# First token tile loaded in two column halves by two queues, and a variance subtraction moved from VectorE to GpSimd, in a fused layer-norm, attention and MLP kernel

## The chip, the cores and the metric

One core of a Trainium2 chip. The time is the device time of one execution in microseconds (us), as the median of several runs. A profile is one execution taken by the hardware profiler; its span is about 1.25 us shorter than that execution's time. All times below that come with no unit are microseconds, and times inside a profile count from the start of its span.

In the lines of profiles, PE is TensorE, PEld its weight loads, DVE VectorE, ACT ScalarE, POOL GpSimd and SPq SyncE's queue. Of the names, `x_tok` holds the token tiles, `bst`, `mv` and `rstd` their statistics, `xnT` the transposed tiles, `WVK` the value weights and `w_s` the MLP weights.

## The reference

```python
def reference(A_x, A_wqkv, A_w_phi, A_wo, B_x, B_w1, B_w3, B_w2):
    x = A_x                                   # [1, 2048, 640], bf16
    xn = _layernorm(x, axis=-1)               # (x - mean) / sqrt(var + 1e-5)
    # _A_ref: qkv projection, 32 heads of 20, a learned feature map with two
    #         softmaxes, linear attention, output projection       ... cut ...
    # _B_ref: (silu(xn w1) * (xn w3)) w2, inner width 1536         ... cut ...
    return x + _A_ref(xn, A_wqkv, A_w_phi, A_wo) + _B_ref(xn, B_w1, B_w3, B_w2)
```

Only the layer norm of the first four token tiles (128 tokens x 640 columns each, 160 KB) and the loads of the first 10 us matter here.

## The kernel before

The kernel is a generator: streams of small steps are emitted in an order chosen from modelled times, and each engine then plays its own list in order, waiting on semaphores. An instruction that waits holds up all that stand behind it on its engine.

The first loads. "SP" is SyncE's queue, "ACT" is ScalarE's. The load of tile 1 reads, in name only, a small zeroed tile, so it waits until VectorE has zeroed it.

```python
    def first_loads():
        load_x(0, 1)                                             # tile 0, SyncE
        o = P.dma("ACT", x_tok[:, 1:2, :], x_t[:, 1:2, :])       # tile 1, ScalarE
        o.reads = P.regions(zero[:])
        P.op("ACT", "activation", [warm[:]], [warm[:]], (warm[:], warm[:], ACT.Exp), cost=1.5)
        load_wv(0, 2)        # value weights, chunks 0 and 1, 320 KB
        load_x(2, 3)         # tile 2
        load_wv(2, 4)        # chunks 2 and 3
        load_wv(4, DC)       # chunk 4, 160 KB
        load_x(3, 4)         # tile 3
        w13(0, 512)          # two loads of 640 KB
        # ... cut ...
```

The statistics of tiles 0, 2 and 3 come from VectorE, those of tile 1 from two ScalarE sums with a mean (`act_mean`) and a subtraction on VectorE. The power for 1/sqrt is GpSimd's.

```python
    def act_rstd(t):
        v, r = mv[:, t, 1:2], rstd[:, t, 0:1]
        small(v, sums[:, 0:1], sums[:, 8:9], ALU.subtract)       # VectorE
        P.op("POOL", "tensor_tensor", [r], [v, mhalf[:, 0:1]], (r, v, mhalf[:, 0:1], ALU.pow), cost=0.6)
```

The order of the first normalisations is also VectorE's order.

```python
        yield lambda: act_sums(1)            # ScalarE
        yield lambda: ln_stats(0, 1)
        yield lambda: act_mean(1)            # VectorE, needs ScalarE's first sum of tile 1
        yield lambda: ln_apply(0, 0, 256)    # tile 0, then its first transposes
        yield lambda: act_rstd(1)
        yield lambda: ln_apply(0, 256, D)
        # ... cut ...
        yield lambda: ln_sums(2, 0)
        yield lambda: ln_apply(1)
        yield lambda: (ln_sums(2, 1), ln_rstd(2, 1))
        yield lambda: ln_sums(3, 0)          # needs tile 3
        yield lambda: ln_apply(2)            # stands behind it
```

The softmax here doesn't subtract the row's maximum and nothing guards it: scores larger than these inputs give would overflow.

## Time and profile before

| | value | where from |
|---|---|---|
| time | 266.33 (266.24 to 266.5) | median of 3 runs |
| span of the profile | 265.1 | page |
| TensorE busy | 260.4, 98% | page |
| first long stretch of TensorE begins | 7.12 | chain of waits |
| first weight load of the MLP (`PS<-xnT,w_s`) | 11.63 | timeline |

The page's first part gives the busy time of each engine; the chain of waits is followed back from the last instruction, so each of its pieces was on the path that set the end. In a timeline line, the brackets at the end give the idle time ahead of an instruction and what ended it; no brackets mean that the engine went straight on. The lines themselves are in the prediction.

### The profile page before, as it was taken

The page shows a single profiled execution, that of the slowest core. Times are in us where ns is not written, and L with a number is a line of the kernel's source. Part 1 is how long each engine was busy: PE and PEld are TensorE (multiplying, and loading weights), DVE is VectorE, ACT ScalarE, POOL GpSimd, SP SyncE. Part 2 cuts the span into 40 slices and gives each one's busy share as a digit, 9 for nine tenths or more (in the row PEclk, how much of TensorE's full clock was granted, in tenths as well). Part 3 has the DMA queues.
Part 4 walks back from the last instruction along what each step waited for, and adds up shares of the span by engine and source line. Part 5 has one row for each costly group of instructions (what it writes and reads, how often), then busy time and mean ns, then how long its engine had stood idle before and what let it go on. Part 6 is the DMA issues. An engine that isn't in the chain of part 4 may idle for free.

```text
span 265.1 us, 4353 instructions
## 1 busy us (share of the span) xinstructions
PE 260.4 (98%) x1716; PEld 141.0 (53%) x1744; DVE 183.0 (69%) x319; ACT 106.9 (40%) x228; POOL 94.4 (36%) x107
## 2 busy tenths in 40 slices
PE   8999999999999999999999999999999999999997
PEld 4655545565558555555545455555544444444773
DVE  4668999999796679989995979897986103221112
ACT  5656988799870445355225245445220000000000
POOL 4311587989995033333330704333420000000000
DMA  7996068923302890445614174366292362461431
GB/s 221 289 315 170 4 157 236 179 52 53 120 2 56 256 213 11 88 73 99 113 27 80 37 123 80 72 123 121 52 110 49 78 149 74 99 198 22 104 124 52
DMA packets 76757, 29.68 MB, mean 112 GB/s; under 512 B 65472, under 2 KB 76736, under 8 KB 76736
## 3 DMA queue, kind: packets, MB, share of 16 engines
q1 hardware_dynamic: 76592, 29.23, 49.3%
q8 instruction: 14, 0.23, 0.4%
q10 hardware_dynamic: 144, 0.16, 0.2%
q14 instruction: 7, 0.06, 0.1%
HBM read 10.84 MB, written 2.62 MB: 51 GB/s over the span
## 4 chain that ended last, share of the span: by engine, by line
PE 95%; DVE 2%; DMA 1%; issue 1%; POOL 0%
PE PS L104 95%; DMA x_tok<-in_A_x_dram 1%; DVE t L104 1%; DVE hT L104 0%; DVE bst L104 0%; POOL rstd L104 0%; DVE mv L104 0%; DVE x_tok L104 0%; DVE xres L104 0%
## 5 line engine op out<-in xcount | busy, mean ns | idle before, releaser
L104 PE MATMUL PS<-xnT,w_s 128*128 128x512 bf16 x464 | 105.5, 379 | 0.9 <-issue 0.2
L104 PEld LDWEIGHTS PS<-xnT,w_s 128*128 128x128 bf16 x480 | 46.2, 98 | 51.4 <-DVE xnT L104 0.3
L104 POOL TENSOR_TENSOR eqt<-eqt,rS 128x600 bf16<-128x600 bf16 (+1 forms) x32 | 41.1, 1305 | 72.4 <-DVE rS L104 72.4
L104 ACT ACTIVATE th<-PS 128x512 f32<-128x512 f32 x48 | 28.6, 596 | 50.7 <-PE PS L104 50.6
L104 PE MATMUL PS<-WVK,xnT 128*128 128x512 bf16 (+4 forms) x255 | 45.1, 329 | 0.3
L104 POOL TENSOR_TENSOR ekt<-ekt,rS 128x640 bf16<-128x640 bf16 x32 | 39.8, 1275 | 4.9 <-DVE rS L104 4.9
L104 DVE SCALAR_TENSOR_TENSOR t<-th,PS 128x512 bf16<-128x512 f32 x48 | 32.0, 668 | 13.7 <-ACT th L104 13.5
L104 PE MATMUL PS<-hT,w_s 128*128 128x512 bf16 x179 | 41.1, 379 | 0.0
L104 ACT ACTIVATE eqt<-PS 128x240 bf16<-128x240 f32 (+1 forms) x96 | 27.2, 348 | 27.7 <-PE PS L104 25.9
L104 PEld LDWEIGHTS PS<-WVK,xnT 128*128 128x128 bf16 x260 | 24.2, 98 | 19.3 <-ACT WVK L104 0.4
L104 DVE SCALAR_TENSOR_TENSOR hT<-t,PS 128x512 bf16<-128x512 bf16 x48 | 33.0, 687 | 1.6
L104 DVE TENSOR_TENSOR xT<-PS,xT 128x512 bf16<-128x512 f32 x15 | 10.1, 685 | 34.7 <-PE PS L104 31.6
L104 PEld LDWEIGHTS PS<-hT,w_s 128*128 128x128 bf16 x180 | 17.6, 98 | 21.3
L104 DVE TENSOR_REDUCE S<-eqt 128x66 f32<-128x1320 bf16 x16 | 24.2, 1514 | 1.4 <-ACT eqt L104 1.4
L104 DVE TENSOR_REDUCE S<-ekt 128x64 f32<-128x1280 bf16 x16 | 23.3, 1455 | 2.2 <-ACT ekt L104 2.2
L104 PE MATMUL PS<-Wqp,xnT 128*128 128x360 bf16 (+1 forms) x160 | 24.3, 299 | 0.1
L104 ACT ACTIVATE ekt<-PS 128x640 bf16<-128x640 f32 x32 | 22.3, 702 | 1.3 <-PE PS L104 0.8
L104 PEld LDWEIGHTS PS<-Wqp,xnT 128*128 128x128 bf16 x160 | 15.1, 98 | 7.1
L104 DVE RECIPROCAL rS<-S 128x64 f32<-128x64 f32 (+1 forms) x32 | 17.9, 560 | 1.1
L104 PE MATMUL PS<-oT,wo_s 128*128 128x512 bf16 x70 | 17.9, 379 | 0.3
L104 DVE TENSOR_TENSOR o_tok<-PS,g_s 128x360 bf16<-128x360 f32 (+1 forms) x32 | 15.7, 491 | 1.1
L104 DVE BATCH_NORM_STATS2 bst<-x_tok 128x6 f32<-128x320 bf16 x30 | 13.9, 481 | 2.8 <-DMA x_tok<-in_A_x_dram 2.4
(55 smaller groups left out, 153.7 us busy)
## 6 DMA issues: line engine op xcount, KB each, us to landing
w_s<-in_B_w_dram SPq DMA_DIRECT2D x6, 640.0 KB, 6.3
x_tok<-in_A_x_dram SPq DMA_DIRECT2D x3, 640.0 KB, 5.2
w_s<-in_B_w_dram SPq DMA_DIRECT2D x1, 1920.0 KB, 8.0
out_dram<-ot SPq DMA_DIRECT2D x3, 640.0 KB, 3.5
wo_s<-in_A_wo_dram SPq DMA_DIRECT2D x1, 800.0 KB, 5.0
WVK<-in_A_wqkv_dram SPq DMA_DIRECT2D x2, 320.0 KB, 3.8
xres<-in_A_x_dram SPq DMA_DIRECT2D x1, 640.0 KB, 4.8
x_tok<-in_A_x_dram SPq DMA_DIRECT2D x3, 160.0 KB, 3.3
```

What stands on the lines that cost most here:

```text
L104: o = _Op(eng, lambda: m(*args, **kw), r, w, cost)
```

## The change

The intent: tile 0 should land sooner if two queues each bring half of its columns, and the power for tile 1 should come sooner if VectorE need not do the subtraction between the two parts of tile 0's normalisation. To free ScalarE's queue for the half, tile 1 moves to SyncE's queue, and the wait for the zeroed tile goes.

```diff
-    zero = new("zero", [128, 128], bf, RT + 2048)
 ...
     def first_loads():
-        load_x(0, 1)
-        o = P.dma("ACT", x_tok[:, 1:2, :], x_t[:, 1:2, :])
-        o.reads = P.regions(zero[:])
+        P.dma("SP", x_tok[:, 0, 0:320], x_t[:, 0, 0:320])
+        P.dma("ACT", x_tok[:, 0, 320:D], x_t[:, 0, 320:D])
+        load_x(1, 2)
         P.op("ACT", "activation", [warm[:]], [warm[:]], (warm[:], warm[:], ACT.Exp), cost=1.5)
         load_wv(0, 2)
         load_x(2, 3)
 ...
     def act_rstd(t):
         v, r = mv[:, t, 1:2], rstd[:, t, 0:1]
-        small(v, sums[:, 0:1], sums[:, 8:9], ALU.subtract)
+        P.op("POOL", "tensor_tensor", [v], [sums[:, 0:1], sums[:, 8:9]], (v, sums[:, 0:1], sums[:, 8:9], ALU.subtract),
+             cost=0.2)
 ...
-        yield lambda: (memset("DVE", zero[:], 0.0), memset("DVE", warm[:], 0.0), first_loads(), consts())
+        yield lambda: (memset("DVE", warm[:], 0.0), first_loads(), consts())
```

## The prediction

> **What bounds the kernel now.** I read the busy shares first, then TensorE's busy time by stretch, then the chain that ended last, then the timeline of the first 12 us engine by engine, and last the packets of the DMA queues. The page says who is full:
>
> ```profile
> span 265.1 us, 4353 instructions
> PE 260.4 (98%) x1716; PEld 141.0 (53%) x1744; DVE 183.0 (69%) x319; ACT 106.9 (40%) x228; POOL 94.4 (36%) x107
> ```
>
> Busy time by stretch (columns: stretch, its length, then PE, weight loads, DVE, ACT, POOL with counts, granted clock, DMA share, GB/s) says where TensorE still has room:
>
> ```profile
> 7.12:11.86 4.74, 4.58 (x42) 3.32 (x43) 3.26 (x11) 3.57 (x10) 1.10 (x2) 1.00 1.18 292
> 11.86:104.00 92.14, 91.62 (x697) 51.73 (x707) 77.28 (x130) 60.27 (x104) 55.88 (x65) 1.00 0.55 135
> 104.00:113.00 9.00, 8.89 (x55) 4.67 (x56) 8.73 (x16) 4.25 (x13) 3.69 (x3) 1.00 0.39 74
> 113.00:263.30 150.30, 149.40 (x897) 78.38 (x909) 90.20 (x153) 34.96 (x97) 30.77 (x24) 1.00 0.44 89
> ```
>
> From 7.12 to 263.3 us TensorE is busy 4.58 + 91.62 + 8.89 + 149.40 = 254.5 of 256.2 us, so this stretch can hardly shorten; it can only begin sooner. Ahead of it is a serial start, which the chain shows (start, length, what):
>
> ```profile
> 0.80 2.57 DMA x_tok<-in_A_x_dram
> ...
> 3.40 0.51 DVE bst L104
> ...
> 4.76 0.58 POOL rstd L104
> ...
> 5.63 0.21 DVE mv L104
> 5.83 0.30 DVE x_tok L104
> ...
> 7.12 4.58 PE PS L104 x41
> ```
>
> Token tile 0 takes 2.57 us from issue to landing, then two statistics, their aggregate, the power on GpSimd, the normalisation in two parts, and transposes. The variance subtraction of tile 1 (0.21 us, 5.63) stands on VectorE between the two parts of tile 0's normalisation. Behind the transposes everything is TensorE. So the change, all of it before 7 us, is worth just what the start at 7.12 moves by. The rest of what matters there, from the timeline:
>
> ```profile
> 3.77 0.74 ACT L104 ACTIVATE xres<-x_tok 128x640 bf16<-128x640 bf16 x1 [0.84 <-DMA x_tok<-in_A_x_dram]
> 5.14 0.19 ACT L104 ACTIVATION_READ_ACCUMULATOR xres<-x_tok 128x1 f32 x1
> 5.91 0.63 POOL L104 TENSOR_TENSOR rstd<-mv,mhalf 128x1 f32<-128x1 f32 x1 [0.58 <-DVE mv L104]
> 6.63 0.43 DVE L104 TENSOR_SCALAR x_tok<-x_tok,mv,rstd 128x640 bf16<-128x640 bf16 x1
> 21.76 0.20 POOL L104 TENSOR_TENSOR rstd<-rstd 128x2 f32<-128x2 f32 x1
> ```
>
> Tile 1's sums come from ScalarE and are complete at 5.14 + 0.19 = 5.33. Its power starts at 5.91 and ends at 6.54; its normalisation starts at 6.63, right as VectorE gets free of the statistics before it (6.23, 0.48 long, overlapped by some 0.08). The last line prices a tiny GpSimd multiply.
>
> **What the Trainium skill says.** "DMA: Bandwidth & Descriptors", section "Issuing engines are not separate DMA queues": DMAs issued by different engines run on the same 16 DMA engines, and two issuers save only issue time. Here an issue takes 0.40 of the 2.57 us, so two halves do not double the rate. The same page, "Queues, rings and completion order": each DMA engine takes turns between the queue rows that have work. The trace agrees; between 2.4 and 2.8 us the SyncE queue (q1) and the ScalarE queue (q10) share:
>
> ```profile
> q1 hardware_dynamic: 62, 0.07, 49.3%
> q10 hardware_dynamic: 48, 0.06, 41.2%
> ```
>
> Counted in steps of 0.1 us, q1 moves 25 and 21 packets at 2.3 and 2.4, alone, and 14, 10, 9 from 2.6 on, beside q10. Tile 0 (128 rows and 16 completion packets, 144) is through at about 2.95 and lands at 3.37, some 0.4 later. "GPSIMD Engine Reference", section "4.1 Engine selection", calls GpSimd about twice as slow as VectorE for two-input elementwise work. At one or two elements per partition the trace shows no such thing: 0.20 us against 0.21. "Perfetto Trace Analysis", section "Identifying the Most-Contended Engine", warns that matmul occupancy is no measure of distance to peak (weight loads here are 53%). That is why I use it only to see gaps.
>
> **The change part by part.** (1) The load in halves. SyncE's half has the same 128 rows at half the bytes; ScalarE's half is issued now at about 0.8 to 0.9, no longer at 1.03, since the wait for the zeroed tile is gone. First packets came 1.0 us after the issue on q1 (0.80 to 1.8) and 1.4 to 1.5 after it on q10 (1.03 to 2.5). So half b's packets should start at about 2.3. By then q1 had moved 41 packets; half a has some 100 left. In sharing, I estimate 22 packets of the smaller size per 0.1 us for each queue: half a is through at 2.3 + 0.45 = 2.75, landing at about 3.17 in place of 3.37, a gain of 0.20. Half b, behind which no tile 1 interferes until half a is done, is through at about 2.9 to 3.0, landing at about 3.35. That is no gain, but the first statistics (3.20 to about 3.70) hide it. So the chain gains 0.20: statistics at 3.20, aggregate at 4.26, power at 4.56, first part of the normalisation at 5.16 in place of 5.36.
>
> (2) Tile 1 moves to SyncE behind half a, issued at about 1.26 and not at 1.03. It no longer has 128 + 16 packets of the value weights beside it, which now queue behind it. From 2.75 to 2.95 it shares with half b, then runs alone at about 30 packets per 0.1 us: done at about 3.36, landing at about 3.78 against 3.77 less a wake-up now. No change, and ScalarE's sums stay at about 5.33. VectorE's mean (needs ScalarE's first sum, 4.61) still runs 4.67 to 4.88, before 5.16: 0.28 us of slack.
>
> (3) The subtraction. VectorE loses it: from the first part to the second the distance falls from 0.39 (5.36 to 5.75) to the 0.27 at which the subtraction followed, a gain of 0.12 on the second part alone: 5.43 against 5.75. GpSimd gains it: sums 5.33, wake-up 0.05, 0.20 for it, 0.09 between dependent instructions (21.45 + 0.22 to 21.76), power 0.57: ready at 6.25 against 6.54. That is 0.29 sooner, but tile 1's normalisation waits for VectorE too, whose order (copy of the transposed chunk, statistics of tile 2, then this) hangs on the first transposes: 0.20 sooner. So it starts at 6.43, and the subtraction's 0.12 is mostly slack: the first matmuls with the value weights (6.37) need the copies of the first chunks, which move by 0.20.
>
> (4) The zeroing (0.11 us at 0.88) is off the path, and ScalarE's table load only starts sooner.
>
> (5) One more issue on SyncE, so all later ones slip by about 0.46 until queues are full: the value weights, w1, w3, and the 7.27 us transposed load (5.51). Bytes are the same and the DMA engines are full from 2.8 to 10.5, so landings hardly move. w3 lands near 11.2 (cumulated bytes, estimate) and is used near 12.9.
>
> Sum at 7.12: -0.20, of which TensorE can take it all: its warm-up matmuls end at 5.46, and the first transposes move from 5.77 to 5.57. 266.33 - 0.20 = 266.1.
>
> **The rivals.** First, half a gains nothing: from 1.8 to 2.3 q1 moved 41 packets in 0.5 us, far below its later rate, so the time is latency and not bytes; with half b interleaved both finish when the whole tile did. Then only the subtraction is left, and the time stays at 266.3. The other way, small packets and an undisturbed q1 give 0.3, limited by the warm-up's end at 5.46: 266.0. Second, tile 1 lands late (issued 0.23 later, two queues ahead). Beyond 0.28 us late VectorE's mean blocks tile 0's normalisation, being ahead of it in order, and the sums reach GpSimd late: the wait moves from tile 0 to tile 1, time 266.3 to 266.5. For it speaks the later issue, against it that q10's packets started slowly anyway. Third, GpSimd is held up by VectorE on the shared port: the power beside a normalisation took 0.63 against 0.55 to 0.57 elsewhere. This costs under 0.1, and 6.25 has 0.15 of room. Fourth, the program orders each engine's instructions by modelled times at build, so 0.2 to 0.5 us of shift may reorder matmul groups, statistics and loads later on. A few visible TensorE gaps sum to 1.7 us after 7.12, so a reorder can save some tenths; a badly placed wait can cost as much or more. That is the larger part of my uncertainty: +-0.5 us.
>
> **Range and chances.** Central -0.2 with 0.15 for the start and 0.5 for reordering gives 266.1, from 265.4 to 266.8. Two per cent is 5.3 us; the whole start up to 7.12 is hardly more, so faster 0.01, same 0.98, slower 0.01.
>
> **What would show it.** Right: first statistics at about 3.2, GpSimd's subtraction of some 0.2 at about 5.4, first transposes at about 5.57, the continuous TensorE stretch at about 6.92, tile 1's first sum at 3.77 +- 0.1. Wrong: statistics still at 3.4 (the halves gain nothing), a VectorE wait for ScalarE ahead of the first normalisation (tile 1 late), a normalisation of tile 1 that waits for GpSimd (the move costs), or TensorE's busy total after the start changing by more than the start moved (reordering).

## The result

| | before | after |
|---|---|---|
| time, median (6 runs each) | 266.33 (266.17 to 266.68) | 267.08 (266.88 to 268.05) |
| span of the profile | 265.1 | 266.8 |
| first weight load of the MLP in the profile | 11.63 | 13.35 |
| from there to the end | 253.44 | 253.46 |

The ratio after to before is 1.0034, 95% interval 1.0016 to 1.0051. A ratio here is the mean time of one kernel's runs over that of the other's of the same rounds, so it is not quite the ratio of the medians quoted. The changed kernel is slower by some 0.8 us, which counts as the same at a limit of 2% but is clear of the noise, and a gain of 0.2 had been expected. The profile after fell on the slowest of the six runs (268.05), so it shows an additional 1 us that most runs do not have; the experiment "the changed kernel again" below separates the two.

I compared the order of the instructions on every engine in the two programs. TensorE's is identical, and the others differ by the diff alone. So nothing was reordered, and the last row of the table says where to look: everything happened before the MLP begins, and the rest of the span has the same length. In all 16 profiles that rest is 253.4 to 253.5. I go by the MLP's first weight load because matmul records can be missing: before, after, e6, e7, e8 and e9 have 1716 of 1744, and the MLP's first matmul is one of the missing, so that its first visible one comes some 0.22 late.

The page after:

```profile
span 266.8 us, 4353 instructions
PE 260.4 (98%) x1716; PEld 140.5 (53%) x1744; DVE 183.0 (69%) x317; ACT 106.9 (40%) x228; POOL 94.6 (35%) x108
```

The busy times are those of before: no engine does more work. TensorE waits longer. The chain of waits after (start, length, what):

```profile
3.71 5.99 DMA x_tok<-in_A_x_dram
9.72 0.49 DVE bst L104
10.21 0.36 DVE x_tok L104
10.61 2.81 PE PS L104 x25
13.43 0.16 issue
13.58 7.98 PE PS L104 x49
```

(The 0.16 of "issue" is the place of the missing record.) Before, the chain ran through tile 0, issued at 0.80, and was on TensorE from 7.12 on. Now it runs through a load issued at 3.71, which is token tile 3, and gets to TensorE at 10.61. VectorE's timeline after:

```profile
3.17 1.02 DVE L104 BATCH_NORM_STATS2 bst<-x_tok 128x6 f32<-128x320 bf16 x2 [2.24 <-DMA x_tok<-in_A_x_dram]
...
5.14 0.64 DVE L104 TENSOR_SCALAR x_tok<-x_tok,mv,rstd 128x256 bf16<-128x256 bf16 x2 [0.19 <-POOL rstd L104]
...
6.50 0.45 DVE L104 TENSOR_SCALAR x_tok<-x_tok,mv,rstd 128x640 bf16<-128x640 bf16 x1
...
9.72 0.49 DVE L104 BATCH_NORM_STATS2 bst<-x_tok 128x6 f32<-128x320 bf16 x1 [2.11 <-DMA x_tok<-in_A_x_dram]
10.13 0.43 DVE L104 TENSOR_SCALAR x_tok<-x_tok,mv,rstd 128x640 bf16<-128x640 bf16 x1
```

The first three lines are as predicted: statistics at 3.17, tile 0's normalisation at 5.14, tile 1's at 6.50. The fourth is the first statistics of tile 3, which wait 2.11 for the load. The fifth, tile 2's normalisation, had its 1/sqrt from GpSimd by 8.23, but stands behind it. In the profile before, the same two were:

```profile
7.64 0.44 DVE L104 BATCH_NORM_STATS2 bst<-x_tok 128x6 f32<-128x320 bf16 x1
8.39 0.45 DVE L104 TENSOR_SCALAR x_tok<-x_tok,mv,rstd 128x640 bf16<-128x640 bf16 x1 [0.31 <-POOL rstd L104]
```

There the statistics of tile 3 did not wait, and the normalisation of tile 2 waited for its 1/sqrt alone.

GpSimd has its new instruction, between VectorE's work and the power:

```profile
5.57 0.25 POOL L104 TENSOR_TENSOR mv<-sums 128x1 f32<-128x1 f32 x1 [0.47 <-DVE x_tok L104]
5.90 0.56 POOL L104 TENSOR_TENSOR rstd<-mv,mhalf 128x1 f32<-128x1 f32 x1
```

It takes 0.25 and holds up nothing. TensorE's timeline, after:

```profile
7.00 0.45 PE L104 MATMUL PS<-ident,x_tok 128*128 128x128 bf16 x5
...
8.88 1.08 PE L104 MATMUL PS<-WVK,xnT 128*128 128x300 bf16 x7 [0.88 <-DMA WVK<-in_A_wqkv_dram]
10.61 0.45 PE L104 MATMUL PS<-ident,x_tok 128*128 128x128 bf16 x5 [0.66 <-DVE x_tok L104]
...
13.35 0.11 PEld L104 LDWEIGHTS PS<-xnT,w_s 128*128 128x128 bf16 x2 [0.28 <-DVE xnT L104]
```

and before:

```profile
8.89 0.45 PE L104 MATMUL PS<-ident,x_tok 128*128 128x128 bf16 x5
...
11.63 0.11 PEld L104 LDWEIGHTS PS<-xnT,w_s 128*128 128x128 bf16 x2 [0.28 <-DVE xnT L104]
```

The transposes of tile 1 are at 7.00, earlier than before (7.12). The transposes of tile 2, at 8.89 before, are at 10.61. The last value weights arrive late too.

What differs on the way to tile 3 is SyncE's queue. Its issues, before (start, length, load):

```profile
1.26 0.41 SPq L116 DMA_DIRECT2D WVK<-in_A_wqkv_dram  x1
...
3.21 0.43 SPq L116 DMA_DIRECT2D x_tok<-in_A_x_dram  x1
```

and after:

```profile
0.80 0.89 SPq L116 DMA_DIRECT2D x_tok<-in_A_x_dram  x2
1.74 0.43 SPq L116 DMA_DIRECT2D WVK<-in_A_wqkv_dram  x1
...
3.71 0.43 SPq L116 DMA_DIRECT2D x_tok<-in_A_x_dram  x1
```

SyncE needs 0.40 to 0.47 to issue one load of 128 rows. With tile 1 in its second place, every later load is issued some 0.5 later. The prediction knew this, and said that it would not matter as the DMA engines were full. Here is how full they were. Columns: stretch, its length, busy time of PE, weight loads, DVE, ACT and POOL with counts, clock, DMA share, GB/s. Before:

```profile
3.00:3.50 0.50, 0.50 (x3) 0.22 (x2) 0.10 (x1) 0.00 (x0) 0.00 (x0) 1.00 0.96 315
3.50:4.00 0.50, 0.50 (x3) 0.15 (x2) 0.47 (x2) 0.23 (x1) 0.00 (x0) 1.00 1.05 379
```

After:

```profile
3.00:3.50 0.50, 0.50 (x3) 0.22 (x2) 0.33 (x1) 0.00 (x0) 0.00 (x0) 1.00 0.99 159
3.50:4.00 0.50, 0.50 (x3) 0.15 (x2) 0.47 (x2) 0.13 (x1) 0.00 (x0) 1.00 0.80 269
```

In this 1 us the DMA engines moved 159 and 269 GB/s in place of 315 and 379. The share in the column before hides most of it (0.99 in the first stretch): it counts the time that packets take, and here few packets took long. For how much moves, the GB/s has to be read, not the share.

From the trace I worked out two more things for this and every later kernel: when a load had landed (the last of the 16 completions that its semaphore waits for), and when the 100th packet of the first value-weights load (320 KB) began, counted in the order of SyncE's queue. Before: 3.52, and tile 3 landed at 7.32. After: 3.89 and 9.69; of the 16 completions of tile 3, 15 were there by 7.73, and a single one came 2 us behind.

### The profile page after: what moved, and what is told of

Its sections match the earlier page's. It is cut to its first block, busy times and chain, and to the rows that moved or that the text cites. A ratio compares the mean times of both kernels' runs of the same rounds, so it can differ in the third digit from the quotient of the medians.

```text
span 266.8 us, 4353 instructions
## 1 busy us (share of the span) xinstructions
PE 260.4 (98%) x1716; PEld 140.5 (53%) x1744; DVE 183.0 (69%) x317; ACT 106.9 (40%) x228; POOL 94.6 (35%) x108
## 4 chain that ended last, share of the span: by engine, by line
PE 94%; DMA 2%; DVE 1%; SPq 1%; issue 1%
PE PS L104 94%; DMA x_tok<-in_A_x_dram 2%; SPq L116 1%; DVE t L104 1%; DVE hT L104 0%; DVE bst L104 0%; DVE x_tok L104 0%; DVE xres L104 0%
```

## The experiments

Of the theories that the expectations tell apart, the main one (A) is that the lost issue place on SyncE's queue makes the loads behind it late, that tile 3 is then late for VectorE, and that the halves and the subtraction cost or gain little. The rivals: the halves themselves disturb the loads; the subtraction on GpSimd costs; the profile after was one unlucky execution; and, later, that the queue on which tile 1 stands matters and not the place (D), or that only the earliest places count (D2). Any other letter in an expectation stands for one of the rivals in this list. All experiments keep the order of every engine's instructions as it was in the kernel they start from, but for the edit shown; a first build of "tile 1 on ScalarE" let the generator reorder TensorE groups, and was rebuilt with the order fixed before it ran. All runs were correct.

A summary. The ratios are to the kernel before, measured in the same batch of rounds, with their 95% intervals. "Tile 3" is its landing; "weights" the start of that 100th packet where I worked it out; "MLP" is the start of the MLP's first weight load; these three are of the one profiled execution of each.

```
label                     from    median  ratio  interval         weights  tile 3  MLP
before (first profile)            266.33                           3.52    7.32   11.63
after (first profile)             267.08  1.0034 1.0016 to 1.0051  3.89    9.69   13.35
e1_again                  after   267.08  1.0031 1.0020 to 1.0043  3.95    8.63   12.29
e2_tile1_scalar           after   267.18  1.0042 1.0027 to 1.0058          7.51   13.63
e3_shift_only             before  266.96  1.0031 1.0019 to 1.0043  3.93    8.86   12.52
e4_sub_only               before  266.28  1.0006 0.9994 to 1.0018  3.50    8.08   11.74
e6_dummy_slot             before  267.14  1.0030 1.0018 to 1.0042  4.16    8.94   12.59
e7_swap                   after   266.92  1.0032 1.0016 to 1.0047          8.63   12.19
e8_tile3_early            after   267.51  1.0057 1.0025 to 1.0089          6.59   12.69
e9_shift_swap_sub         before  266.61  1.0014 1.0001 to 1.0027  3.95    8.67   11.91
e10_before_sub_swap       before  266.49  1.0008 0.9996 to 1.0020          7.18   11.82
e11_tile1_gpsimd          after   268.04  1.0074 1.0048 to 1.0100          7.44   12.63
e12_slot_before_tile3     before  266.27  1.0002 0.9989 to 1.0015  3.47    7.61   11.54
e13_slot_after_tile3      before  266.17  0.9999 0.9987 to 1.0011  3.46    7.16   11.48
e14_weights_scalar        after   266.98  1.0021 1.0007 to 1.0034          7.54   12.29
e15_slot_after_weights    before  266.69  1.0019 1.0006 to 1.0032  3.48    7.78   11.53
```

### The changed kernel again (e1_again)

No edit.

> The changed kernel again, unaltered, for a second profile. Theory A (queue slot): one more load on SyncE makes every later load on that queue start one slot (about 0.46 us) later, and the last value-weight chunk and token tile 3 land after their users ask for them. Then the slip is there again: tile 3 lands 7.6 us or later (7.3 in the kernel before), VectorE waits for it ahead of tile 3's statistics, and the time is 266.8 to 267.2. Theory B (one stray run): the 1.5 to 2 us by which the last of the 16 completions of these two loads lagged in the first profile is chance; then most runs are near 266.3 and the new profile shows no wait for a load after 7 us. Theory C (the halves or the move to GpSimd are slow in themselves): the first statistics or tile 1's normalisation are later than before; the first profile already speaks against it (3.17 against 3.40, 6.50 against 6.63).

Measured: 267.08 (266.35 to 267.32), ratio 1.0031. VectorE again waits for tile 3, now 0.99 and not 2.11:

```profile
8.65 0.49 DVE L104 BATCH_NORM_STATS2 bst<-x_tok 128x6 f32<-128x320 bf16 x1 [0.99 <-DMA x_tok<-in_A_x_dram]
```

TensorE's wait of 0.88 for the value weights is gone. So the loss of 0.8 is there in ordinary runs and comes with the wait for tile 3. The further 1 us of the first profile goes with the straggling completion of tile 3: it landed 1.06 later there than here (9.69 against 8.63), and the MLP began 1.06 later (13.35 against 12.29).

### Only the move of tile 1 to SyncE's second place (e3_shift_only)

```diff
 (before)
         load_x(0, 1)
-        o = P.dma("ACT", x_tok[:, 1:2, :], x_t[:, 1:2, :])
-        o.reads = P.regions(zero[:])
+        load_x(1, 2)
```

> The kernel before with one alteration: tile 1 is issued by SyncE as its second load and not by ScalarE. No halves, subtraction on VectorE. Theory A: the slot alone costs, 0.4 to 1.0 us: 266.7 to 267.3, with a wait for tile 3 or the value weights after 7 us. Theories B and C: as before, 266.2 to 266.5.

Measured: 266.96 (266.77 to 267.2), ratio 1.0031: the whole loss, with tile 0 in one piece and the subtraction on VectorE. VectorE waits for the same load:

```profile
8.88 0.49 DVE L104 BATCH_NORM_STATS2 bst<-x_tok 128x6 f32<-128x320 bf16 x1 [1.58 <-DMA x_tok<-in_A_x_dram]
```

The gap in the transfers is plainest here. GB/s from 3.0 to 3.5 us in 40 slices of 12.5 ns, e3:

```profile
GB/s 410 102 205 103 0 205 103 0 0 0 102 0 0 102 102 0 0 0 0 0 0 0 0 0 102 0 0 0 102 0 102 0 102 0 102 0 0 0 205 0
```

and before:

```profile
GB/s 205 307 308 205 307 307 410 102 205 410 308 205 103 614 205 410 102 205 307 307 205 205 410 205 410 103 615 103 717 102 512 205 820 102 307 410 717 205 307 410
```

In e3 the data of tiles 0 and 1 are through by about 3.05, and the weights, issued 0.46 later than before, have hardly begun: zeros for most of the stretch, 54 GB/s on average. Before, not one slice is empty. (A packet counts where it begins. The engines had packets in hand in the empty slices: of those that SyncE's queue began from 2.8 to 3.3 in e3, nine took 0.41 to 1.16 each, where most take 0.06; before, the longest from 2.9 to 3.4 took 0.30. Why they took so long isn't shown.)

This run also says something about the halves: with the whole tile, statistics began at 2.94, earlier than in any profile with halves (3.04 to 3.34).

### Only the subtraction on GpSimd (e4_sub_only)

```diff
 (before)
-        small(v, sums[:, 0:1], sums[:, 8:9], ALU.subtract)
+        P.op("POOL", "tensor_tensor", [v], [sums[:, 0:1], sums[:, 8:9]], (v, sums[:, 0:1], sums[:, 8:9], ALU.subtract),
+             cost=0.2)
```

> The kernel before with the subtraction on GpSimd and nothing else. Theory A: no loss; tile 1's power is ready sooner and the second part of tile 0's normalisation about 0.1 sooner, of which little reaches the end: 266.2 to 266.35. Theory C (GpSimd's part): 266.6 or more, with tile 1's normalisation waiting for GpSimd beyond 6.7.

Measured: 266.28 (265.88 to 266.64), ratio 1.0006, interval around 1. The subtraction neither costs nor gains anything that can be seen. Its profile has tile 3 at 8.08, late for a kernel with before's loads, and VectorE waits 0.37 for it; but the MLP begins at 11.74, only 0.11 later than before. So most of a wait of a few tenths for tile 3 is absorbed by the work that TensorE still has in hand.

### Tile 1 on ScalarE's queue, behind its half (e2_tile1_scalar)

```diff
 (after; issued by ScalarE, at 1.23)
-        load_x(1, 2)
+        o = P.dma("SP", x_tok[:, 1:2, :], x_t[:, 1:2, :])
+        o.emit, o.part = (lambda: nc.scalar.dma_start(x_tok[:, 1:2, :], x_t[:, 1:2, :])), "A"
```

> The changed kernel, but tile 1 is issued by ScalarE right behind its half of tile 0, so SyncE's loads keep the slots they had before. All else, the order of instructions on every engine too, is that of the changed kernel. Theory A: the gain of the start (0.1 to 0.2 us) is kept and no load is late: 266.1 to 266.3, value weights and tile 3 landing at about 7.0 and 7.3 as before. Theory B: about as the repeat of the changed kernel run beside it. Theory C: as slow as the changed kernel, 266.8 to 267.2.

Measured: 267.18 (266.79 to 268.32), ratio 1.0042; the profiled execution was the slowest. SyncE's places are those of before again (weights at 1.26), and tile 3 lands at 7.51, in time, as A says. The time is nevertheless no better, which A did not expect. The new wait:

```profile
6.25 0.21 DVE L104 TENSOR_SCALAR sums<-mv 128x1 f32<-128x1 f32 x1 [1.85 <-ACT xres L104]
```

(Left out of this cut: the line that sends the issue to ScalarE's list.) Tile 1 now shares the DMA engines with the value weights and lands at 5.36 (before: 3.75). VectorE's mean of tile 1 waits for ScalarE's first sum, and stands ahead of tile 0's normalisation; the first transposes slip to 6.77. TensorE then also ran slower for a while: its next four matmuls with the value weights took 1.25, where the same four took 0.72 in e11 after a similar wait; no run here shows why. This is the second rival of the prediction, tile 1 late. The change itself didn't have it, this repair does.

### A spare load in SyncE's second place (e6_dummy_slot)

```diff
 (before)
+    pad = new("pad", [128, 16], bf)
 ...
         P.op("ACT", "activation", [warm[:]], [warm[:]], (warm[:], warm[:], ACT.Exp), cost=1.5)
+        P.dma("SP", pad[:], x_t[:, 15, 0:16])
         load_wv(0, 2)
```

> The kernel before with one small load (128 rows of 32 bytes, to a spare tile) put into SyncE's second slot. Tile 1 stays on ScalarE, nothing is in halves; only the slots of the later SyncE loads slip by about 0.46 us. Theory A (the slot makes tile 3 late for VectorE, whose order has tile 3's first statistics ahead of tile 2's normalisation): tile 3 lands 0.4 to 0.6 later than in the kernel before, at 7.7 to 8.5, and the time is 266.5 to 267.0. Theory D (not the slot but tile 1 in the same queue makes the later loads late: one queue where there were two): tile 3 lands at about 7.3 to 7.5 and the time stays at 266.1 to 266.4.

Measured: 267.14 (266.66 to 267.38), ratio 1.0030. The load is 4 KB in rows of 32 bytes, used by nothing; tile 1 stays on ScalarE's queue, tile 0 is whole. It costs as much as the whole change, a little more than A expected (266.5 to 267.0, tile 3 by 8.5; it landed at 8.94):

```profile
8.96 0.49 DVE L104 BATCH_NORM_STATS2 bst<-x_tok 128x6 f32<-128x320 bf16 x1 [1.23 <-DMA x_tok<-in_A_x_dram]
```

From 3.0 to 4.0 the DMA engines moved 100 and 133 GB/s. So the place in the queue costs, not what is in it, and D (the queue of tile 1) falls. A reservation: its 128 small packets take DMA time too (the later runs with the same load in other places show how little).

### Tile 2's normalisation ahead of tile 3's statistics (e7_swap, e9_shift_swap_sub, e10_before_sub_swap)

If VectorE's order turns a late tile 3 into a late tile 2, the order can be changed. The edit moves one instruction, at the time when the lists are made:

```diff
         nc = self.nc
+        def nth(name, n, eng=None):
+            return [i for i, o in enumerate(self.ops) if o.name.startswith(name) and eng in (None, o.eng)][n]
+        i, j = nth("bn_stats:", 4), nth("tensor_scalar:x_tok", 3, "DVE")
+        self.ops.insert(j, self.ops.pop(i))
```

e7 is the changed kernel with this. e9 is e3 with this and the subtraction on GpSimd; e10 is before with this and that subtraction.

> The changed kernel with two VectorE instructions in the other order: tile 2's normalisation goes ahead of tile 3's first statistics. All loads as in the changed kernel. Theory A and D alike (the loss is VectorE held up by tile 3's load in order): tile 2's normalisation starts at 8.2 to 8.4, TensorE's third group of transposes at 8.7 to 8.9, time 266.0 to 266.4, although tile 3 still lands at 7.7 or later. If the loss lay in late weights or elsewhere: 266.8 to 267.2 as before the swap.

> The candidate: tiles 0 and 1 both whole, both issued by SyncE (as in the run with the shift only, where tile 0 landed at 2.92), with the swapped VectorE order and the subtraction on GpSimd. If whole tiles land no later than halves and the wait for tile 3 was all that was lost: 265.7 to 266.1, faster than the kernel before by 0.1 to 0.5. If the slot costs elsewhere as well (weights): 266.3 or more.

> The candidate for a kernel that beats both: the loads of the kernel before, the subtraction on GpSimd, tile 2's normalisation ahead of tile 3's first statistics on VectorE. In the run with the subtraction only, VectorE still waited 0.37 us for tile 3 (landed 8.08). If that wait reaches the end: 265.9 to 266.2 here, against 266.2 to 266.3 of the kernel before. If not: the same within 0.1.

Measured: e7 266.92 (266.82 to 268.14), ratio 1.0032; e9 266.61 (266.54 to 266.79), 1.0014; e10 266.49 (266.37 to 266.52), 1.0008. All three missed what was expected: 266.0 to 266.4 for e7, 265.7 to 266.1 for e9, and for e10 265.9 to 266.2, or the same within 0.1. In e7's profile tile 1 happened to land at 4.25 (3.85 in the first profile after, 3.58 in e1), which delayed the mean to 5.14. Then tile 2's normalisation begins at 8.61, without a wait for tile 3, and TensorE's transposes of it are at 9.12 and not at 9.55 as in e1; but the statistics of tile 3, now behind it, keep VectorE until 10.2, and the copies of the transposed tile 2 stand behind these. TensorE waits there:

```profile
10.45 1.25 PE L104 MATMUL PS<-WVK,xnT 128*128 128x300 bf16 x8 [0.16 <-DVE xnT L104]
```

e10 has no late tile and shows that same wait of 0.16, at 10.08: the swap itself has this price. e9 against e3 is a gain of 0.35 in the medians, with intervals that overlap, so the swap may repair a part of the loss; it doesn't bring it below before. The transposes of tile 2 in e3 and then in e9, although tile 3 landed no sooner than 8.67 in either:

```profile
9.78 0.45 PE L104 MATMUL PS<-ident,x_tok 128*128 128x128 bf16 x5 [0.75 <-DVE x_tok L104]
...
8.95 0.44 PE L104 MATMUL PS<-ident,x_tok 128*128 128x128 bf16 x5
```

The fairest test of the blocking by order is e9 against e10, which differ by the move of tile 1 alone. With the swap, that move costs 0.12 in the medians (1.0014 and 1.0008, intervals that overlap almost wholly). Without it, e3 against e4 (which differ by the subtraction too, shown above to cost nothing), it costs 0.68 (1.0031 and 1.0006, intervals that don't overlap). The swap's own price, 0.21 from e4 to e10, hid this. So most of the loss seems to pass through VectorE's order; the kernels were timed in three batches and their medians lie only tenths apart, so a share of it can't be given.

### Tile 3 loaded sooner (e8_tile3_early)

```diff
 (after; the order of SyncE's loads: ..., tile 2, tile 3, value weights 2-3, 4)
+        i, j = nth("dma:x_tok", 4), nth("dma:WVK", 1)
+        self.ops.insert(j, self.ops.pop(i))
```

> The changed kernel with tile 3 loaded right behind tile 2, ahead of the second and third load of value weights. Theory A: tile 3 lands at 6.0 to 6.8, VectorE does not wait; but the last value weights land some 0.5 later (7.5 to 8), near to when TensorE asks for them at about 7.7, so the time is 266.1 to 266.6. If tile 3's lateness is not what costs: 266.8 to 267.2.

Measured: 267.51 (266.83 to 270.17), ratio 1.0057; A expected 266.1 to 266.6 and missed. Tile 3 lands at 6.59 and nobody waits for it. Now the last value weights land at 9.00 (6.89 before), and TensorE waits for those:

```profile
9.04 1.08 PE L104 MATMUL PS<-WVK,xnT 128*128 128x300 bf16 x7 [0.47 <-DMA WVK<-in_A_wqkv_dram]
```

So the lateness isn't a property of tile 3. The loads behind the lost place are late as a row; moving one forward moves the lateness to another.

### The spare load in later places (e12_slot_before_tile3, e13_slot_after_tile3, e15_slot_after_weights)

The same 4 KB load as in e6, in the kernel before: e15 in SyncE's third place (behind the first value weights), e12 in its sixth (just ahead of tile 3), e13 in its seventh (just behind tile 3). In e12 and e15 the list is edited as above; e13 reads (with `pad` as in e6):

```diff
         load_x(3, 4)
+        P.dma("SP", pad[:], x_t[:, 15, 0:16])
         w13(0, 512)
```

> The kernel before with the same small spare load, now in SyncE's slot just ahead of tile 3's, so that the value weights keep their slots and only tile 3 and the later loads slip by about 0.46 us. Theory A (each slot ahead of tile 3 delays tile 3, and VectorE waits in order): tile 3 lands at 7.8 or later and the time is 266.5 to 267.1, about as with the spare load in the second slot (267.14). Theory D2 (what costs is that the queue has nothing for the DMA engines between 3.0 and 3.5 us, when the slot comes early; later the engines have a backlog that hides a slot): tile 3 lands at 7.3 to 7.6, time 266.1 to 266.5.

> The kernel before with the spare load in SyncE's slot behind tile 3's, ahead of w1. Theories A and D2 alike: nobody waits for what slips (w1 lands at 9.9 and is used at 11.9), time 266.1 to 266.4. A time of 266.7 or more would say that the later loads (w1, w3, the transposed load) are what costs, and not tile 3 or the value weights.

> The kernel before with the spare load in SyncE's third slot: behind the first value weights (still issued at 1.26), ahead of tile 2 and all others. If only a slot ahead of the first weights starves the DMA engines: no gap at 3.0 to 4.0 us, tile 3 by 7.7, time 266.1 to 266.4. If any early slot does: 266.6 to 267.2, as with the second slot (267.14).

Measured: e15 266.69 (266.23 to 267.24), ratio 1.0019; e12 266.27 (266.24 to 266.35), 1.0002; e13 266.17 (266.07 to 266.44), 0.9999. With e6 this is a series: the same load in the second, third, sixth and seventh place costs 0.30%, 0.19%, 0.02% and nothing. In e12 the load for tile 3 is issued one place later, as in the changed kernel, yet VectorE goes straight on:

```profile
7.63 0.49 DVE L104 BATCH_NORM_STATS2 bst<-x_tok 128x6 f32<-128x320 bf16 x1
```

That corrects A: it isn't that tile 3 is issued 0.46 later. A place counts as long as the DMA engines have no backlog, and by the sixth place there is one: so says D2, whose expectation was met, though the backlog itself wasn't measured. It also weakens the reservation on e6: in the sixth and seventh place the small packets cost nothing that shows.

e15 fits in kind: the weights begin on time (3.48), 3.0 to 4.0 is full, and the gap comes one load later:

```profile
4.00:4.50 0.50, 0.50 (x4) 0.29 (x3) 0.47 (x2) 0.50 (x3) 0.00 (x0) 1.00 1.20 245
4.50:5.00 0.50, 0.50 (x10) 0.50 (x8) 0.24 (x2) 0.50 (x1) 0.37 (x1) 1.00 0.76 185
```

Before, these two moved 376 and 289. But its profiled execution was its fastest (266.23), with a wait of only 0.18 for tile 3 (7.78). The slower ones, up to 267.24, have no profile, so what they waited for isn't shown.

### Tile 1 from GpSimd's queue, and the weights from ScalarE's (e11_tile1_gpsimd, e14_weights_scalar)

Two more attempts to keep the halves and give SyncE its places back. e11 issues tile 1 from GpSimd, by the same edit as in e2 with `nc.gpsimd`. e14 leaves tile 1 in SyncE's second place and lets ScalarE issue the first value weights behind its half, at 1.23:

```diff
 (after, e14)
-        load_wv(0, 2)
+        o = P.dma("SP", WVK[:, 0:2, 0:D], wqkv_t[:, 0:2, 2 * D:3 * D])
+        o.emit, o.part = (lambda: nc.scalar.dma_start(WVK[:, 0:2, 0:D], wqkv_t[:, 0:2, 2 * D:3 * D])), "A"
```

> The changed kernel with tile 1 issued by GpSimd as its first work, a third queue, so that SyncE's loads have the slots of the kernel before; all orders else as in the changed kernel. If the slot is the whole loss and tile 1 lands by 4.3: 266.0 to 266.4. If tile 1 comes late again, as it did on ScalarE behind the half (5.36): VectorE's mean of tile 1 holds up tile 0, and the time is 266.6 to 267.3. The halves themselves gain nothing in either case: whole tiles landed at 2.92 to 3.38, halves at 3.05 to 3.32.

> The changed kernel with the first load of value weights issued by ScalarE right behind its half (at about 1.25, where SyncE issued it in the kernel before), so that no slot ahead of the others is lost and tile 1 stays SyncE's second. If the gap in the DMA engines' work between 3.0 and 4.0 us, which comes from the first weights being issued at 1.74 and not 1.26, is the cause: 280 GB/s or more in both halves of that stretch (changed kernel 159 and 269, repeat 154 and 205), tile 3 landing by 7.6, VectorE not waiting for it, time 266.0 to 266.4. The risk: tile 1 shares the engines with these weights and lands after 4.3, then VectorE's mean of tile 1 blocks and the time is 266.5 to 267. If the gap is not the cause: 266.8 to 267.2.

(Left out again: the lines that send the issue to ScalarE's list and move it ahead of ScalarE's own work.)

Measured: e11 268.04 (267.2 to 269.77), ratio 1.0074, of which the three runs at a clock of 1.0 took 267.2 to 267.54; e14 266.98 (266.42 to 267.13), 1.0021. In both tile 3 is in time (7.44 and 7.54) and VectorE doesn't wait for it. e14 filled the gap only in part: 220 and 287 GB/s in the two halves of 3.0 to 4.0, where 280 or more was expected in both. In both kernels tile 1 is late, at 5.03 and 4.69, and the mean waits as in e2, 1.60 in e11 and in e14:

```profile
5.58 0.21 DVE L104 TENSOR_SCALAR sums<-mv 128x1 f32<-128x1 f32 x1 [1.19 <-ACT xres L104]
```

Together with e2 that is three repairs in which the wait for tile 3 vanishes, as A says it must when the weights are issued early, and a wait for tile 1 comes in its place.

## Why the prediction was wrong

It said 266.1, 265.4 to 266.8; the median was 267.08. By its own steps:

**Part (5) failed.** "One more issue on SyncE, so all later ones slip by about 0.46 until queues are full" was right. "Bytes are the same and the DMA engines are full from 2.8 to 10.5, so landings hardly move" was wrong, and is the term of the sum that was left at zero and measured +0.8. The engines were full in the profile before because the weights had been issued at 1.26. A 160 KB tile per 0.46 us issue is 356 GB/s (163,840 bytes / 0.46 us), about what the DMA engines moved when busy (315 to 379). So, by this estimate, SyncE's queue is fed a tile about as fast as it drains one and builds no stock; a load of weights brings 320 KB in one issue and builds some. By 1.7 us the kernel before had issued tile 0, tile 1 from the other queue, and 320 KB of weights: 640 KB. The changed one had issued two halves and tile 1: 320 KB. w3, which the prediction put near 11.2, landed at 11.79 before and at 13.36 after; as the MLP slid too, nothing waited for it. Fullness seen in a profile was taken for a property of the chip's load, when it was made by the order that the change alters. The spare load shows that the place is the cause (e6), its series of places that it counts only early (e15, e12, e13), and e3 that nothing else of the change is needed.

**From the gap to the loss.** The weights start 0.37 to 0.64 later in after, e1, e3 and e6 and landed at 5.30, 5.62, 5.37 and 5.75 (4.66 before), all behind them is late, and VectorE, in order, waits for tile 3 ahead of tile 2's normalisation. The prediction never asked when tile 3 was needed: in the profile before it landed at 7.32 and was used at 7.64, so the slack was 0.32. That number was in the profile. The blocking by order is seen in the profiles of after, e1, e3 and e6. Undoing it brought tile 2's transposes forward but paid a price of its own (e7, e9); net of that price, e9 against e10, little of the loss is left.

**Part (1), the halves: right about the step, wrong about its worth.** Statistics were expected at 3.20 and began at 3.17. That is partly luck: ScalarE's packets, expected from 2.3, began at 1.82, and in e1, the same kernel, statistics began at 3.34. And the 3.40 of the profile before was a late draw. A whole tile 0 landed at 2.92 to 3.38 over nine profiles; over the seven with halves, SyncE's half, which the first statistics need, landed at 3.01 to 3.32 and the later of the two at 3.15 to 3.32. So no gain from halves shows. The first rival said this. The statement of the Trainium skill that the prediction used ("DMA: Bandwidth & Descriptors", "Issuing engines are not separate DMA queues", that several issuers share the same DMA engines) agrees: no doubling.

**Part (2), tile 1 on SyncE: right.** Its first sum began at 3.87 (predicted 3.77 plus or minus 0.1), and the mean didn't hold up tile 0. The second rival did not happen in the changed kernel's first profile; in e7, which has the same loads, it did (tile 1 at 4.25, the mean at 5.14).

**Part (3), the subtraction: right.** 0.25 on GpSimd (0.20 predicted), at 5.57 (about 5.4 predicted), and tile 1's normalisation at 6.50 (6.43 predicted). e4 confirms that it moves nothing that can be seen in the time. GpSimd's power after it took 0.56 and no longer stood beside a normalisation, so the third rival, GpSimd held up by VectorE, had no room to show.

**The fourth rival**, a reordering at build, was held to be the larger part of the uncertainty. The order was unchanged. The 1.7 us of visible TensorE gaps that it named were mostly missing matmul records: from 7.12 to 263.3 TensorE shows 254.49 busy in the profile before, with 28 records missing, and 255.95 in e13, with none missing. The uncertainty was real and sat elsewhere.

**What stays open.** Why one of the 16 completions of a load sometimes comes late: 2.0 behind the 15th for tile 3 and 1.5 for the last value weights in the first profile after, 0.7 for tile 1 in e7 (15 by 3.57, the last at 4.25). Why a slip of 0.46 at the issue becomes a loss of 0.8, that is, why tile 3 is 1.3 or more later in the profiles of e1, e3 and e6 than before's 7.32. The first of its 16 completions came 0.37 to 0.53 after before's 6.43 in after, e1, e3 and e6, about the slip of the issue; the rest is that the 16 lie further apart. They do so in e4 too (6.46 to 8.08), which has before's loads. Why e15's slower runs are slow. And how much of e7's and e9's misses is the varying landing of tile 1. No version here beats the kernel before; its arrangement (tile 1 alone on ScalarE's queue, weights second on SyncE's) is better balanced than it looks.

## What to carry to other kernels

Before adding a DMA issue to the front of a queue, count the bytes issued by each moment against what the DMA engines move: where the two rates are about equal, there is no stock, and one issue more can delay every load behind it, whatever it carries. "The DMA engines are full" is true of the profile it was read from only; for each load that slips, compare its landing with its first use, and look at what stands behind that use on the same engine. Don't take one profile's landing time as the value of a change that is smaller than the spread of landings.

## What the Trainium skill lacked or had wrong

- "DMA: Bandwidth & Descriptors", "Issuing engines are not separate DMA queues": it says that issuing from several engines saves only issue time, "which is usually small relative to the DMA itself". In this start it isn't small in effect: one issue of 0.41, of a load of 4 KB, in SyncE's second place cost 0.9 us (267.14 against 266.25, e6), and the same in the sixth place nothing (e12).
- I found on no page used here how much later a load lands when it shares the DMA engines with a larger one from another queue: tile 1 landed at 3.75 alone on ScalarE's queue (before), and at 5.36, 5.03 and 4.69 when it was issued with or behind the halves and beside the weights (e2, e11, e14).
- "GPSIMD Engine Reference", "4.1 Engine selection": twice as slow as VectorE for two-input elementwise work, which it says of a tile, doesn't show at one element per partition: 0.19 to 0.27 on GpSimd against 0.21 on VectorE for the same subtraction, and no change of the time (e4).
